# A written-out sequence in place of a priority planner: attention and linear attention, one core

## The chip, the cores and the metric

One core of one Trainium2 chip runs the whole kernel. The time is device microseconds of one execution, from its first instruction to its last; the median of several executions is given, with the lowest and the highest. A separate execution is taken by the hardware profiler, and all durations of single instructions come from that one. The engines are PE (TensorE, matmuls, with its weight loads shown as PEld), ACT (ScalarE), DVE (VectorE), POOL (GpSimd) and SP (SyncE, here only an issuer of DMA transfers).

## The reference

Two independent blocks, A and B, each take x (2048 rows, 640 columns, bf16) and weights wqkv (640 x 1920) and wo (640 x 640); their outputs are put side by side.

```python
# A: causal attention in a window of 256, 32 heads of 20
q, k, v = split(x @ wqkv)
scores = einsum("bhqd,bhkd->bhqk", q, k) * 20 ** -0.5
scores = where((i - j >= 0) & (i - j < 256), scores, -1e9)
a = (softmax(scores) @ v) @ wo
# B: linear attention, 32 heads of 20
phi = lambda t: where(t > 0, t + 1, exp(t)) + 1e-6
kv = einsum("bhsd,bhse->bhde", phi(k), v);  z = phi(k).sum(s)
b = (phi(q) @ kv / (phi(q) @ z + 1e-6)) @ wo
out = concatenate([a, b], axis=-1)
```

## The kernel before

The rows are cut into four tiles t of 512. For A and each t, the program makes q, k and v: `q{t}.{i}` and `k{t}.{i}` are groups of five matmuls of 512 columns (i from 0 to 4), `v{t}.{b}.{i}` are groups of five matmuls of 320 columns for each block b of 128 rows and each half i. The five matmuls of a group run over five pieces of 128 of the inner dimension, in order, and add up in one PSUM buffer F; there are four such buffers. An evacuation, named `.ev`, copies the finished buffer to SBUF, on ACT or on DVE.

The first tile of A is special. Its x is loaded row by row in four blocks, `x0n0` to `x0n3`, and PE transposes them (`x0t0` to `x0t3`, five matmuls each); v of block b needs only x0t{b}. Its weights come in pieces of 128 rows: `ld.wv0` to `ld.wv4` go straight to where they are used; `ld.wq0..4` and `ld.wk0..4` land in wqn and wkn and are rearranged by copies `cq0..5` and `ck0..5`. So matmul number c of a v group of this tile waits for wv{c}, and that of a q or k group for cq{c} or ck{c}. Before the data come, PE runs warm-up matmuls (`warm`, one piece of five with 512 columns and eight of two with 256). All later x tiles come by a transposing DMA (`ldxA1`, `ldxB0` and so on).

Attention of A goes by units `S{t}.{g}.{u}`: scores of eight heads go into the only score buffer S (four banks), ACT turns them into p by one exp `E{t}.{g}.{u}` (128 x 2048, in four cases 128 x 1536), DVE multiplies the edges by a mask (`M`), and after the units of a g, one `PV{t}.{g}` forms p times v in two F buffers. There are 76 units. The result goes to DRAM (`ow`), comes back turned (`oc`, and the sums `osum`), is normalised (`ln`, `rec`, `nrm`) and multiplied by wo (`oa{t}.{b}.{half}`), and stored. q and k also need copies of their heads in other partitions, which POOL's queue makes (`rl1`, `rl2`); v needs swapped halves (`sw`), by SP's queue.

B's work fills PE between the units: keys `kB{t}.{b}.{half}`, the sums `G` (16 matmuls each), `z`, `kv`, `kvwo`, and then queries `qB{t}.{c}`, denominators `den{t}` and outputs `ob{t}.{b}.{half}`. A last `flag` matmul counts bad sums; the engines read the flag at the very end and branch.

What sets the order. The function `build` only declares operations (some 2,080), each with the engines that could run it, a duration, its dependencies, a priority and, for some, an earliest time. The class `Planner` then plays this program through at build time: its `run` takes, again and again, the engine that is free first, and on it the ready operation of lowest rank; the operation is emitted there. PE's, ACT's, DVE's, POOL's and SP's streams and the one named ACTQ, transfers issued by ACT, are planned as six separate queues, although ACT and ACTQ are one stream of instructions on the chip. The priorities and the earliest times come from a table `TUNE` of numbers, the settings from `PRM`. Which of ACT and DVE does an evacuation also falls out of this play. On the chip, every engine then works its stream in order and waits on semaphores.

In order of issue the queues begin so, before:

- SP: wk2, wk1, x0n3, wq3, x0n2, wq1, x0n0, wv1, wq0, wq4, wq2, wv3, x0n1, xtok0, woA, wk0, wk4, wk3, ldxA1
- ACT: wv0, wv2, wv4 (loads), then the copies ck2, ck1, cq3, cq1, cq0, cq4, cq2
- PE: nine pieces of warm-up, x0t3, v0.3.1 (first matmul), v0.3.0, x0t2, v0.2.1, x0t0, and so on; all 40 v matmuls, 25 of q and 14 of k stand ahead of the first scores

Of the kernel before, what the change touches and what calls it, by code (L numbers as in the profile page):

```python
# [11 lines left out]
F32 = mybir.dt.float32  # L12
I32 = mybir.dt.int32
INF = 1 << 40
PRM = {"rq": "POOL", "pvw": 2854, "look": 13955, "slack": 991, "xm": 5, "sq": "SP"}
TUNE = {
# [49 lines left out]
}  # L66


def KEY(name, value):
# [25 lines left out]
ENGS = ["PE", "ACT", "DVE", "POOL", "SP", "ACTQ"]  # L95
# [5 lines left out]
class Planner:  # L101
# [54 lines left out]
                o.left += 1  # L156
            o.ready = {e: o.earliest for e in o.engs}

    def run(self, dry=False):
        self.prepare()  # L160
        avail = {e: [] for e in ENGS}
        for o in self.ops:
            if o.left == 0:
# [2 lines left out]
        free = self.free  # L166
        while True:
# [12 lines left out]
            t, e = best  # L180
# [6 lines left out]
            o = pick[1]  # L187
# [26 lines left out]
            done = t + dur  # L214
# [1149 lines left out]
```

## Time and profile before

| what | us |
|---|---|
| median of three runs | 260.22 |
| lowest, highest | 259.57, 260.45 |
| the profiled execution | 261.95 |
| its span, first to last instruction | 260.4 |
| PE busy | 245.7 |
| ACT busy | 198.6 |
| DVE busy | 181.5 |
| mean granted PE clock | 0.99 |

A row of the timeline has the start and the length in us, the engine, the line, the operation with what it writes and reads, the number of instructions merged into it, and in brackets the idle time before it and what ended that. SPq and ACTq are the issuing of transfers by SP and ACT. A row of the windows has the stretch, then for each engine its busy time and count, the granted PE clock (1.00 is full), the busy share of the DMA engines and GB/s. A group's row has its busy time, the mean length of one, the idle time before and what ended most of it. Line numbers of the program after the change are 70 higher in most of the file: line 416 becomes 486, 472 becomes 542, 568 becomes 638.

### The profile page before, as it was taken

The page shows a single profiled execution, that of the slowest core. Times are in us where ns is not written, and L with a number is a line of the kernel's source. Part 1 is how long each engine was busy: PE and PEld are TensorE (multiplying, and loading weights), DVE is VectorE, ACT ScalarE, POOL GpSimd, SP SyncE. Part 2 cuts the span into 40 slices and gives each one's busy share as a digit, 9 for nine tenths or more (in the row PEclk, how much of TensorE's full clock was granted, in tenths as well). Part 3 has the DMA queues.
Part 4 walks back from the last instruction along what each step waited for, and adds up shares of the span by engine and source line. Part 5 has one row for each costly group of instructions (what it writes and reads, how often), then busy time and mean ns, then how long its engine had stood idle before and what let it go on. Part 6 is the DMA issues. An engine that isn't in the chain of part 4 may idle for free.

```text
span 260.4 us, 9473 instructions
## 1 busy us (share of the span) xinstructions
PE 245.7 (94%) x4094; PEld 145.5 (56%) x4126; DVE 181.5 (70%) x458; ACT 198.6 (76%) x205; POOL 40.5 (16%) x93
## 2 busy tenths in 40 slices
PE   7699999999999999899999999999899999999993
PEld 4353455545555666545556666665545565556572
DVE  0456768978879987777778353459978777867831
ACT  4412789979789989977897778879979899756831
POOL 8000560009306300116041000000000000000000
PEclk9999999999999999999999999999979999999998
DMA  6769962786297816652457060662859223125133
GB/s 205 227 208 197 255 86 64 201 187 193 64 142 178 192 54 196 144 144 58 127 158 144 15 183 13 160 206 54 241 150 216 103 86 111 34 82 176 52 120 116
DMA packets 51828, 36.07 MB, mean 139 GB/s; under 512 B 31862, under 2 KB 50374, under 8 KB 51782
## 3 DMA queue, kind: packets, MB, share of 16 engines
q1 hardware_dynamic: 49302, 32.31, 47.0%
q0 software_dynamic: 2048, 2.63, 5.5%
q8 instruction: 33, 0.54, 0.9%
q10 hardware_dynamic: 432, 0.49, 0.7%
q14 instruction: 13, 0.11, 0.1%
HBM read 13.90 MB, written 10.26 MB: 93 GB/s over the span
## 4 chain that ended last, share of the span: by engine, by line
PE 79%; DMA 6%; ACT 5%; issue 3%; DVE 3%; SPq 2%; DVEq 0%
PE F L726 17%; PE F L507 14%; PE S L638 10%; PE F L864 9%; PE F L839 8%; PE F L1021 7%; PE F L568 7%; PE F L692 7%; ACT p L654 3%; DMA wkn<-in_A_wqkv_dram 2%; DMA wqn<-in_A_wqkv_dram 2%; PE F L1033 1%; DMA wv<-in_A_wqkv_dram 1%; ACT e L800 1%; SPq L1164 1%
## 5 line engine op out<-in xcount | busy, mean ns | idle before, releaser
L654 ACT ACTIVATE p<-S 128x2048 bf16<-128x2048 f32 x76 | 141.1, 1856 | 25.3 <-PE S L638 23.2
L666 DVE TENSOR_TENSOR p<-p,strip 128x256 bf16<-128x256 bf16 (+2 forms) x140 | 49.2, 379 | 9.5 <-ACT p L654 9.2
L800 ACT ACTIVATE e<-F 128x320 bf16<-128x320 f32 (+1 forms) x52 | 25.3, 500 | 5.8 <-PE F L1021 5.1
L416 DVE CAST even<-F 128x512 bf16<-128x512 f32 x30 | 20.7, 689 | 12.9 <-PE F L507 10.0
L839 PE MATMUL F<-wkB,xT 128*128 128x320 bf16 x160 | 27.9, 300 | 0.3 <-issue 0.2
L568 PE MATMUL F<-wv,xT 128*128 128x320 bf16 x160 | 26.3, 300 | 1.7 <-DVE xT L416 1.2
L538 POOL DMA_DIRECT2D odd<-even x32 | 17.0, 538 | 68.6 <-DVE even L416 30.1
L726 PE MATMUL F<-woA,oc 128*128 128x320 bf16 x160 | 26.5, 302 | 0.0
L1021 PE MATMUL F<-xT,wqB 128*128 128x512 bf16 x91 | 25.1, 394 | 1.1 <-issue 0.5
L507 PE MATMUL F<-xT,wk 128*128 128x512 bf16 x89 | 23.9, 380 | 1.4 <-issue 0.8
L416 DVE CAST osb<-F 128x320 bf16<-128x320 f32 x38 | 18.1, 486 | 10.2 <-PE F L726 9.8
L726 PE MATMUL F<-kvwo,pq 128*128 128x320 bf16 x160 | 24.9, 299 | 0.2 <-DVE p L666 0.2
L507 PE MATMUL F<-xT,wq 128*128 128x512 bf16 x92 | 24.0, 379 | 0.5 <-issue 0.3
L864 PE MATMUL F<-pk,xtok 128*128 128x320 bf16 x160 | 24.3, 300 | 0.0
L541 POOL DMA_DIRECT2D odd<-st x32 | 17.8, 562 | 27.3 <-DVE st L416 12.0
L692 PE MATMUL F<-p,sw 64*32 64x320 bf16 (+3 forms) x720 | 21.1, 254 | 0.0
L692 PE MATMUL F<-p,vt 64*32 64x320 bf16 (+3 forms) x720 | 21.0, 254 | 0.0
L416 DVE CAST ost<-F 128x512 bf16<-128x512 f32 x22 | 14.6, 687 | 8.8 <-PE F L692 8.7
L568 PEld LDWEIGHTS <-xT 128*128 128x128 bf16 x160 | 14.8, 98 | 9.6 <-DVE xT L416 1.8
L839 PEld LDWEIGHTS <-xT 128*128 128x128 bf16 x160 | 14.7, 98 | 9.0 <-issue 1.0
L726 PEld LDWEIGHTS <-oc 128*128 128x128 bf16 x160 | 15.1, 99 | 8.2 <-issue 1.3
L726 PEld LDWEIGHTS <-pq 128*128 128x128 bf16 x160 | 15.3, 98 | 7.8 <-issue 0.6
(87 smaller groups left out, 300.0 us busy)
## 6 DMA issues: line engine op xcount, KB each, us to landing
out_dram<-osb SPq DMA_DIRECT2D x32, 160.0 KB, 2.0
OD<-ost SPq DMA_DIRECT2D x32, 128.0 KB, 2.1
xtok<-in_B_x_dram SPq DMA_DIRECT2D x4, 640.0 KB, 5.3
oc<-OD SPq DMA_DIRECT2D x4, 640.0 KB, 4.3
odd<-even POOLq DMA_DIRECT2D x32, 48.0 KB, 3.8
sw<-vt SPq DMA_DIRECT2D x16, 87.0 KB, 2.7
odd<-st POOLq DMA_DIRECT2D x32, 32.0 KB, 2.9
wkn<-in_A_wqkv_dram SPq DMA_DIRECT2D x5, 160.0 KB, 5.8
```

The source lines that it names most:

```text
L416: nc.vector.tensor_copy(out=dst, in_=src)
L507: nc.tensor.matmul(ps[:, a:b], lhsT=w[:, kt, i, :], rhs=xb["t"][:, kt, a:b], start=(kt == 0), stop=(kt == KT - 1))
L568: return lambda ps: nc.tensor.matmul(ps[:], lhsT=xb["t"][:, kt, bb * P : bb * P + P], rhs=rhs_(), start=(kt == 0), stop=(kt == KT - 1))
L638: nc.tensor.matmul(st["s"][64 * i : 64 * i + 64, o0 : o0 + b - a], lhsT=kb["t"][32 * j : 32 * j + Dh, sl, ko : ko + 64], rhs=qb["t"][32 * ...
L654: nc.scalar.activation(out=o_, in_=i_, func=ACT.Exp, scale=scale)
L666: nc.vector.tensor_tensor(out=x, in0=x, in1=mkv[:, None, :].to_broadcast([P, 4, 64 * w]), op=ALU.mult)
L692: nc.tensor.matmul(O[i][32 * j : 32 * j + 32, a:b], lhsT=lhsT, rhs=pb["t"][64 * i : 64 * i + 64, o0 : o0 + b - a], start=(cnt == 0), stop= ...
L726: return lambda ps: nc.tensor.matmul(ps[:], lhsT=lhs(c), rhs=rhs(c, hf), start=(c == 0), stop=(c == KT - 1))
L800: nc.scalar.activation(out=eb["t"][:, 0:n], in_=ps[:], func=ACT.Exp)
L839: return lambda ps: nc.tensor.matmul(ps[:], lhsT=xb["t"][:, kt, b * P : (b + 1) * P], rhs=R["wkB"][:, kt, hf * HALF : (hf + 1) * HALF], st ...
L864: return lambda ps: nc.tensor.matmul(ps[:], lhsT=R["xt", tb // 4][:, tb % 4, c * P : (c + 1) * P], rhs=R["pk", tb // 4][:, tb % 4, hf * HA ...
L1021: return lambda ps: nc.tensor.matmul(ps[:], lhsT=R["wqB"][:, kt, :].rearrange("p (f c) -> p c f", c=KT)[:, c, :], rhs=xb["t"][:, kt, :], s ...
```

## The change

`PRM` and `TUNE` lose their contents (the settings fall back to defaults that are the same where they matter for what is built), and a list `SEQ` of 2,084 numbers comes in. Each number is an operation and its engine: `word // 8` is the operation's place in the order of declaration, `word % 8` the queue. A new method `follow` walks the list and emits each operation there; `run` calls it instead of the play. Which of the buffers F, O or L an operation gets now goes by who gave one back first in the list.

```diff
-PRM = {"rq": "POOL", "pvw": 2854, "look": 13955, "slack": 991, "xm": 5, "sq": "SP"}
-TUNE = {
-    "x0n0": -496785, "@x0n0": 5831, "x0n1": -176047, "@x0n1": 11250, "x0n2": -3061, "@x0n2": 4097, "x0n3": 93019, "@x0n3": 43, "ld.wv0": 41152,
...
-}
+PRM = {"sq": "SP"}
+TUNE = {}
+SEQ = [
+    100, 109, 32, 0, 368, 378, 141, 16, 40, 56, 24, 84, 76, 64, 336, 116, 132, 1344, 8, 188, 92, 212, 346, 196, 220, 320, 156, 330, 48, 281, 1136,
...
+]
...
+    def follow(self, dry):
+        done = set()
+        free = {}
+        for k in self.slots:
+            free.setdefault(k[0], []).append(k)
+        for word in SEQ:
+            o, e = self.ops[word // 8], ENGS[word % 8]
+            assert o.left == 0 and e in o.engs and o.idx not in done, o.name
+            done.add(o.idx)
+            if o.acq:
+                g, (n, kind) = o.acq
+                assert len(free[kind]) >= n, o.name
+                g["slot"] = [free[kind].pop(0) for _ in range(n)]
+            o.eng = e
+            if not dry:
+                o.emit(e)
+            self.log.append(o)
+            for g, i in o.rel:
+                free[g["slot"][i][0]].append(g["slot"][i])
+            for s in o.succ + o.osucc:
+                s.left -= 1
+        assert len(done) == len(self.ops)
+
     def run(self, dry=False):
         self.prepare()
+        if SEQ:
+            return self.follow(dry)
```

The operations are the same ones. What the list says, engine by engine:

- SP begins with x0n3, x0n1, x0n0, wv1, wv3, wk0, x0n2, wk3, wk1, wk4, wq1, wk2, wq0, wq3, wq4, wq2, ldxA1, sw0.0 (two), sw0.1, ldxB0, wkB; xtok0 and woA come later.
- ACT begins with the loads wv0 and wv4, the copy ck1, the load wv2, and then ck4 and evacuations; the other copies of wq and wk but cq4 are now DVE's.
- PE begins with a short piece of warm-up, the five long matmuls, x0t3, five short pieces, x0t1, v0.3.1 (first matmul), one piece, x0t0, one piece, v0.1.1, v0.3.1, v0.1.1, v0.0.0 (two), and then the third matmul of v0.3.1. Groups are mixed more finely: neighbours on PE belong to different groups 668 times, before 401 times. Ahead of the first scores stand 35 v matmuls and 35 of q and k.
- ACT has 214 operations and DVE 429, before 203 and 440: 80 evacuations and small operations stood on ACT between the exps, now 99.
- The flag matmul stands last on PE; before, 67 matmuls stood behind it.

140 rows, old and new, of tables (SEQ, TUNE) are left out of this document.

## The prediction

> **What bounds the kernel now.** I read the page's parts 1 and 5 first, then five-microsecond windows, then the timelines of the first 14 us and of the exps, and last the end of the chain.
>
> ```profile
> PE 245.7 (94%) x4094; PEld 145.5 (56%) x4126; DVE 181.5 (70%) x458; ACT 198.6 (76%) x205; POOL 40.5 (16%) x93
> ...
> L654 ACT ACTIVATE p<-S 128x2048 bf16<-128x2048 f32 x76 | 141.1, 1856 | 25.3 <-PE S L638 23.2
> ```
>
> ```profile
> 0.00:5.00 5.00, 3.51 (x12) 1.76 (x13) 0.28 (x2) 2.27 (x4) 3.86 (x24) 1.00 0.55 159
> 5.00:10.00 5.00, 2.99 (x26) 1.96 (x25) 0.98 (x2) 1.68 (x3) 1.84 (x5) 1.00 0.77 256
> 10.00:15.00 5.00, 4.23 (x36) 2.72 (x35) 2.78 (x8) 2.77 (x6) 0.00 (x0) 1.00 0.83 245
> ...
> 145.00:150.00 5.00, 5.00 (x149) 3.34 (x150) 1.99 (x6) 4.15 (x3) 0.00 (x0) 1.00 0.02 3
> ```
>
> PE is busy for 94% of the span. Of its 14.7 us idle, 4.3 lie in the first 15 us, and 4.1 behind its last matmul. In the middle two things run at the same pace: PE, and the ring scores, exp, next scores, since there is one score buffer. Its timeline:
>
> ```profile
> 26.21 1.88 ACT L654 ACTIVATE p<-S 128x2048 bf16<-128x2048 f32 x1 [0.67 <-PE S L638]
> 28.88 1.88 ACT L654 ACTIVATE p<-S 128x2048 bf16<-128x2048 f32 x1 [0.79 <-PE S L638]
> 31.45 1.88 ACT L654 ACTIVATE p<-S 128x2048 bf16<-128x2048 f32 x1 [0.70 <-PE S L638]
> ```
>
> An exp of 1.88 us and a gap of about 0.74, so 2.62 us per unit of scores. The gap takes one or two evacuations on ACT for nothing; a third costs time. The head:
>
> ```profile
> 1.38 0.06 DVE L437 MEMSET tiny<- 128x1 f32 x1
> ...
> 1.50 0.87 ACTq L472 DMA_DIRECT2D wv<-in_A_wqkv_dram  x2
> ...
> 2.40 0.45 ACTq L472 DMA_DIRECT2D wv<-in_A_wqkv_dram  x1
> ...
> 3.35 0.62 ACT L414 COPY wk<-wkn 128x512 bf16<-128x512 bf16 x1 [0.81 <-DMA wkn<-in_A_wqkv_dram]
> 4.83 0.33 SPq L1093 DMA_DIRECT2D x0n<-in_A_x_dram  x1
> 4.83 0.62 ACT L414 COPY wk<-wkn 128x512 bf16<-128x512 bf16 x1 [0.87 <-DMA wkn<-in_A_wqkv_dram]
> ...
> 7.38 0.33 SPq L472 DMA_DIRECT2D wv<-in_A_wqkv_dram  x1
> 7.41 0.45 PE L1126 MATMUL F<-ident,x0n 128*128 128x128 bf16 x5 [0.84 <-DMA x0n<-in_A_x_dram]
> ```
>
> and, from the chain that ended last, one load from its issue to its landing:
>
> ```profile
> 9.18 2.95 DMA wv<-in_A_wqkv_dram
> ```
>
> Three things are to be seen. First, loads are issued in order and held: the third x load went out when wk1 landed (SP and ACT both at 4.83), the next wv load when the first x load landed (7.38 and 7.41); the eight transfers in flight are reused in turn. Second, ACT's loads stand in ACT's own stream: they left at 1.50, when tiny was written (1.38 + 0.06), while SP issued from 1.04. Third, the first transfer issued landed at 3.35, the second at 4.75, the third of SP's queue at 7.4.
>
> **The change, part by part.** The page's execution took 261.95 us (span 260.4, 1.55 around it), 1.7 above the median of 260.22. I sum against the span and put the difference on the median.
>
> *Head.* x0n3, x0n1, x0n0 go first on SP, then wv1, wv3, wk0, x0n2, wk3, wk1. ACT issues wv0 and wv4 at once. But on ACT the copy ck1 of wk1 now stands ahead of the load of wv2, and every group of v needs wv2 as the third of its five weight pieces. PE takes its queue in order: three transposed blocks and six v matmuls, then v0.3.1's third, which waits for wv2. So:
> - x0n0, third on SP, lands at 6.7 to 7.4 (the row of 7.41, with one transfer less on ACT's queue).
> - wk1 reuses the place of x0n0, so it goes out then. A load issued at 7.75 landed by 10.21 (ACT's copy of wq0), the one at 9.18 in 2.95 us. wk1 lands at 9.7.
> - wv2 is issued at 9.75 and lands 2.95 us later: 12.7. Bounds: 11.9 with a landing of 2.3 us (the first load's, alone) and wk1 at 9.6; 14.2 with 4.4 (x0n1's under load).
> - From there to the first scores PE has 5 transposes, 29 v matmuls and 35 of q and k: 5 x 0.06 + 29 x 0.136 + 35 x 0.216 = 11.8 us (spacings from the runs of 11 at 12.17 and of 20 at 17.75), plus 0.3 of waits, as before's same stretch had (11.04 of work in 11.34).
> - Clock. PE stands still from about 9.5 to 12.7. The nearest row is the one place where PE was underused later:
>
> ```profile
> 189.00:190.00 1.00, 0.61 (x10) 0.25 (x17) 1.00 (x4) 1.00 (x3) 0.00 (x0) 1.00 0.39 133
> 190.00:191.00 1.00, 1.00 (x26) 0.54 (x23) 1.00 (x5) 1.00 (x3) 0.00 (x0) 0.54 0.00 0
> 191.00:192.00 1.00, 1.00 (x3) 0.29 (x2) 1.00 (x3) 1.00 (x1) 0.00 (x0) 0.50 0.58 137
> ```
>
> After 3.4 us with PE at 0.59 to 0.85 the granted clock was half for 3.4 us, which costs 1.7. The other bound is 0: from 7 to 10, at 0.41 to 0.56 busy, no drop shows. A PE that does nothing is nearer to the first, less what passes before wv2 lands: 1.6. First scores at 12.7 + 11.8 + 0.3 + 1.6 = 26.4, against 25.7: **+0.7**.
> The Trainium skill's page TensorE: Matmul & The Clock Gate (What's actually happening) says that the clock halves after at least one idle window of about 3.4 us, on a free-running grid. The row above dropped without an idle window. By the page a stop of 3.2 us need hold no whole window, and the head would be -0.9 instead of +0.7; that is rival 2.
>
> The other loads moved: xtok0 and woA leave the head (they put wk's last pieces at 16.00, which cost PE only a wait of 0.36). The first transposing load, whose issue holds SP for 5.55 us, now follows wq2 at about 11, and sw0.0, ldxB0 and wkB queue behind it. wkB then lands near 28; its first matmul stands four units, 10 us, behind the first scores. Nothing on the path; bounds 0 and the 0.36. POOL's relays keep their number and go by the evacuations; DVE's ck5 and cq5 (1.2 each) are done 8.7 us behind wv2, and q0.4 asks for them at 11.6: hidden, 0.
>
> *Middle.* From first to last scores there are 75 units. For each I take the larger of the PE work standing between its scores and the next, and 1.88 (1.45 for the four short exps) plus the larger of 0.74 and ACT's other work between the two exps, at the rows' durations less 0.05 each for overlap. Before this sums to 200.5 where the trace has 224.2 - 25.7 = 198.5, so it is fair to 1% and the bias is common. After, it sums to 203.2: **+2.7**. The terms: PE work 190.3 to 193.2, as five v matmuls and some of k0 move behind the first scores and work comes forward from the end; ACT's work between exps 40.3 to 48.8, as 19 more evacuations of 0.43 to 0.58 move there. DVE loses 7 us there, but at 70% it bounds nothing. Bounds for what such a sum can't see (a buffer freed late, a mask behind a waiting evacuation): -2 (nearly half of the 5.8 us of PE idle in before's middle gone) and +3 (each t losing as much as S3.1 did over its sum, 0.6, and one dip of the clock more). I take 0, as before's sixteen groups of units each came out within 0.6 of the sum.
>
> *End.* PE work from the last scores on falls from 31.6 to 30.2: **-1.4**. The flag matmul moves from 246.9 to PE's very end: 0.17 of PE, 0.15 and 0.14 of DVE, and SP's read of 0.54. The last evacuation (0.43) and store issue (0.4) take as long, and SP reads the flag behind them anyway: 0, at most 0.3.
>
> Sum: 0.7 + 2.7 - 1.4 = **+2.0 us**, or 262.2 on the median. The break-even is first scores at 24.4.
>
> **The rivals.**
> 1. *wv2 does not wait.* If a load on ACT leaves without waiting for ck1, or ck1 is early, wv2 goes out at 2.40 as the third load of before did and lands by 8.0 (5.6, the longest landing of a wv load there). PE reaches that point at about 9.4 (strip is ready at 3.1, then five warm-up matmuls of 0.43, ten of 0.1 to 0.2, three blocks), first scores at 9.4 + 12.1 = 21.5: -4.2 + 2.7 - 1.4 = -2.9, 257.3. For: x and wv do lead the queues. Against: the 1.50 row. It decides once wv2 lands before 10.7 at half clock or 12.3 at full clock. Then the change would have done what its words say; by my reading four of five pieces of wv lead, and the fifth does not.
> 2. *The clock stays up*, as it did from 7 to 10 with PE at 0.41 to 0.56. Against: here PE does not run at all, and 190 shows that less was enough. Head -0.9, sum +0.4, 260.6: within 0.3% (0.8 us, about what a measurement of this kernel can tell from no change).
> 3. *The middle suffers more.* ACT's added evacuations hold the ring and buffers beyond the sum, +2 to +3: about 264.5. For: two gaps with three evacuations, where before has none. Against: PE's queue is spaced to 2.6 us there.
> 4. *The middle gains* the -2 above, with PE's stall at 186 to 190 and its clock dip gone: 260.2, or faster with an early wv2.
>
> **Chances.** Forecast 0.46; rival 1 0.20; rival 2 0.13; rival 3 0.12; rival 4 0.09, shared between same and faster. Rival 2 also spills over to faster with wv2 at 11.9. Hence faster 0.28, same 0.14, slower 0.58. The range for 8 in 10 is 257.2 to 264.4, from rival 1 to rival 3; the forecast's own is 261.0 to 263.6.
>
> **What would show it.** On ACT the load of wv2 starts at 9.5 or later, right when wk1 lands; PE idle 2.5 us or more ahead of a v matmul (F<-wv,xT) that waits for DMA wv; a granted clock of half in the slices behind it; first scores at 25 to 27.5, last scores near 228; ACT's idle ahead of the exps down from 25 by about 6; and PE's last matmul 32 us behind the last scores. An ACT load of wv2 issued before 3 us, or first scores before 23, would make me wrong in the head; 75 units taking under 199 or over 204 us, in the middle.

## The result and the profile after

| | before | after |
|---|---|---|
| median, us | 259.89 (258.89 to 260.45, four executions) | 272.32 (271.54 to 273.88, four executions) |
| the profiled execution, its span | 261.95, 260.4 | 271.54, 270.0 |

The changed kernel takes 1.049 times as long (95% interval 1.043 to 1.056): slower, by 12.4 us where the prediction had 2.0 and a range that ended at 264.4. The page's part 1 and its group of the exps, after:

```profile
PE 246.4 (91%) x4097; PEld 146.3 (54%) x4126; DVE 176.6 (65%) x447; ACT 200.8 (74%) x216; POOL 40.9 (15%) x93
...
L724 ACT ACTIVATE p<-S 128x2048 bf16<-128x2048 f32 x76 | 141.2, 1858 | 21.9 <-PE S L708 19.0
```

The engines have little more work: PE went from 245.7 to 246.4 us, ACT from 198.6 to 200.8. Of the 9.7 us of span, 9.0 are idle time of PE (14.7 before, 23.6 after). ACT's idle time ahead of the exps (the number behind the second bar) fell from 25.3 to 21.9 all the same. I cut both spans at three marks (first exp, last exp, end of PE's last matmul):

| stage, us | before | after | difference |
|---|---|---|---|
| start to first exp | 26.21 | 26.46 | +0.25 |
| first to last exp (75 units) | 198.55 | 203.26 | +4.7 |
| last exp to PE's end | 31.5 | 30.6 | -1.0 |
| PE's end to the span's end | 4.1 | 9.8 | +5.7 |

The spans differ by 9.7 us, the medians by 12.4. The execution profiled before was 2.1 us longer than the median of its kernel. It holds the stretch at half clock at 190 that the prediction shows; two other executions of this order or nearly this order, without such a stretch, took 197.0 and 196.8 us from first to last exp (the order before written out, and the flag late, in the table below). Against those the middle lost 6.3 us, not 4.7. The execution profiled after was the shortest of its four, 0.8 below their median; where the others lost more was not profiled.

**Head.** From the timeline after (start, length, engine, line, operation, count, idle time before it and what ended it):

```profile
6.15 2.34 PE L1139 MATMUL F<-strip,ident 128*128 128x256 bf16 x10
9.12 0.62 ACT L484 COPY wk<-wkn 128x512 bf16<-128x512 bf16 x1 [6.59 <-DMA wkn<-in_A_wqkv_dram]
9.13 0.35 ACTq L542 DMA_DIRECT2D wv<-in_A_wqkv_dram  x1
9.63 4.85 SPq L553 DMA_TRANSPOSE xT<-in_A_x_dram  x1
14.10 1.66 PE L638 MATMUL F<-wv,xT 128*128 128x320 bf16 x11 [3.45 <-DMA wv<-in_A_wqkv_dram]
26.46 1.88 ACT L724 ACTIVATE p<-S 128x2048 bf16<-128x2048 f32 x1 [1.31 <-PE S L708]
```

The wait is where the prediction put it: the load of wv2 leaves with the copy that waits for wk1, and PE stands 3.45 us for it. Eleven matmuls in 1.66 us, 0.136 apart, are full speed: the clock did not fall here. The +0.25 at the first exp is less than this mark varies by: in three other executions with the same head (flag early, the two swap runs) it came at 25.8, 25.2 and 27.7. Part of that is PE's warm-up. The ten small matmuls at 6.15 took 2.34 us here, 0.21 apart, and 1.34 us, 0.11 apart, in others, while the windows show a granted clock of 1.00 for both.

**Middle.** Nearly all of the +4.7 lies in one place. The timeline of 99 to 112:

```profile
99.43 1.88 ACT L724 ACTIVATE p<-S 128x2048 bf16<-128x2048 f32 x1
99.66 0.44 SPq L927 DMA_DIRECT2D xtok<-in_B_x_dram  x1
100.60 0.65 SPq L653 DMA_DIRECT2D sw<-vt  x1
101.97 1.88 ACT L724 ACTIVATE p<-S 128x2048 bf16<-128x2048 f32 x1
103.03 2.86 SPq L553 DMA_TRANSPOSE xT<-in_A_x_dram  x1
105.85 0.49 DVE L486 CAST vt<-F 128x320 bf16<-128x320 f32 x1 [3.88 <-DMA sw<-vt]
106.40 0.43 PE L909 MATMUL F<-wkB,xT 128*128 128x320 bf16 x2 [2.72 <-DVE vt L486]
107.26 1.88 ACT L724 ACTIVATE p<-S 128x2048 bf16<-128x2048 f32 x1 [3.08 <-PE S L708]
111.85 1.88 ACT L724 ACTIVATE p<-S 128x2048 bf16<-128x2048 f32 x1 [0.67 <-PE S L708]
```

The exps are 2.54 apart until 101.97, and then 5.29 and 4.59. DVE's cast at 105.85 is the evacuation of the v group v2.1.0. It waits 3.88 us for a transfer that reads the tile it writes, the second half of the swap `sw2.0`, issued at 100.60; PE waits behind the cast, and the scores behind PE. The chain that ended last gives the transfer's time, and that of the late load in the head:

```profile
9.13 4.92 DMA wv<-in_A_wqkv_dram
...
100.60 5.16 DMA sw<-vt
```

In the kernel before, the evacuation of v2.1.0 was planned ahead of both halves of that swap; in the written list the second half stands ahead of it. By the code the two do not even touch the same columns (the swap's half reads columns 336 to 683 of both blocks, the evacuation writes into columns 0 to 335 of the second), but the program makes the later one in the list wait. The second long gap, 4.59, is mostly the clock (in the run with the flag early, where the wait was shorter and the clock stayed up, it was 3.37). Windows of 1 us (stretch, busy time and count of PE, PEld, DVE, ACT and POOL, granted clock, share of the DMA engines, GB/s):

```profile
107.00:108.00 1.00, 0.90 (x20) 0.44 (x5) 1.00 (x4) 0.74 (x1) 0.00 (x0) 0.90 1.17 355
108.00:109.00 1.00, 0.58 (x3) 0.20 (x2) 0.96 (x3) 1.00 (x1) 0.82 (x2) 0.50 0.12 42
109.00:110.00 1.00, 1.00 (x6) 0.52 (x5) 0.52 (x2) 0.20 (x2) 1.00 (x3) 0.50 0.36 57
110.00:111.00 1.00, 1.00 (x5) 0.56 (x4) 0.55 (x2) 0.64 (x2) 1.00 (x3) 0.50 0.66 90
```

**The span's end.** PE's last matmul, the flag's, is issued at 260.12. What reads its result, by the views of the flag's tile and of the lines that use it (lengths in ns, least, median and most, then the starts of first and last), after:

```profile
L1276 DVE CAST fint<-fsum x1: 141/141/141, 260.5 to 260.5; 1x1 int32<-1x1 f32 x1
L1288 POOLq TENSOR_LOAD <-fint x1: 770/770/770, 260.7 to 260.7; - x1
L1289 POOLq INC_SWDGE_SEM  x1: 1471/1471/1471, 262.4 to 262.4; - x1
L1429 POOLq DRAIN  x3: 34/107/5288, 263.9 to 269.8; - x3
```

and the same before:

```profile
L1206 DVE CAST fint<-fsum x1: 141/141/141, 247.8 to 247.8; 1x1 int32<-1x1 f32 x1
L1218 POOLq TENSOR_LOAD <-fint x1: 491/491/491, 248.0 to 248.0; - x1
L1219 POOLq INC_SWDGE_SEM  x1: 1471/1471/1471, 249.5 to 249.5; - x1
L1359 POOLq DRAIN  x3: 34/107/5288, 251.0 to 260.1; - x3
```

POOL reads the flag, branches, spends 1.47 us on one instruction and 5.29 us in a DRAIN. Before, it began this at 248.0 and its long DRAIN was over at 256.3, with PE's last matmul. After, it begins at 260.7 and nothing covers it.

### The profile page after: what moved, and what is told of

Its sections match the earlier page's. It is cut to its first block, busy times and chain, and to the rows that moved or that the text cites. A ratio compares the mean times of both kernels' runs of the same rounds, so it can differ in the third digit from the quotient of the medians.

```text
span 270.0 us, 9475 instructions
## 1 busy us (share of the span) xinstructions
PE 246.4 (91%) x4097; PEld 146.3 (54%) x4126; DVE 176.6 (65%) x447; ACT 200.8 (74%) x216; POOL 40.9 (15%) x93
## 4 chain that ended last, share of the span: by engine, by line
PE 76%; DMA 8%; ACT 5%; DVE 4%; issue 2%; SPq 1%; DVEq 0%; ACTq 0%
PE F L796 16%; PE F L577 15%; PE S L708 9%; PE F L638 8%; PE F L909 7%; PE F L1091 7%; PE F L934 5%; PE F L762 5%; DMA sw<-vt 3%; ACT p L724 3%; DMA wv<-in_A_wqkv_dram 2%; PE F L1103 2%; DMA x0n<-in_A_x_dram 1%; DMA wkn<-in_A_wqkv_dram 1%; DVE p L736 1%
## 5 line engine op out<-in xcount | busy, mean ns | idle before, releaser
L724 ACT ACTIVATE p<-S 128x2048 bf16<-128x2048 f32 x76 | 141.2, 1858 | 21.9 <-PE S L708 19.0
L736 DVE TENSOR_TENSOR p<-p,strip 128x512 bf16<-128x512 bf16 (+2 forms) x140 | 49.7, 382 | 18.7 <-ACT p L724 18.3
L909 PE MATMUL F<-wkB,xT 128*128 128x320 bf16 x160 | 32.8, 308 | 3.3 <-DVE vt L486 2.7
L638 PE MATMUL F<-wv,xT 128*128 128x320 bf16 x160 | 31.1, 300 | 3.6 <-DMA wv<-in_A_wqkv_dram 3.5
L796 PE MATMUL F<-woA,oc 128*128 128x320 bf16 x160 | 30.6, 303 | 0.6 <-ACT osb L484 0.5
L577 PE MATMUL F<-xT,wk 128*128 128x512 bf16 x91 | 26.7, 380 | 0.7 <-issue 0.5
L796 PE MATMUL F<-kvwo,pq 128*128 128x320 bf16 x160 | 27.3, 299 | 0.1
L577 PE MATMUL F<-xT,wq 128*128 128x512 bf16 x92 | 26.8, 380 | 0.3
L608 POOL DMA_DIRECT2D odd<-even x32 | 17.1, 541 | 58.3 <-ACT even L484 39.4
L486 DVE CAST ost<-F 128x512 bf16<-128x512 f32 x28 | 18.5, 685 | 9.2 <-PE F L762 9.0
L638 PEld LDWEIGHTS <-xT 128*128 128x128 bf16 x160 | 14.7, 98 | 12.3 <-issue 4.7
L874 DVE TENSOR_SCALAR e<-e 128x320 bf16<-128x320 bf16 (+1 forms) x52 | 13.5, 259 | 10.8 <-ACT e L870 9.9
L486 DVE CAST even<-F 128x512 bf16<-128x512 f32 x21 | 14.5, 688 | 8.7 <-PE F L577 8.0
```

What stands on the lines that cost most here:

```text
L486: nc.vector.tensor_copy(out=dst, in_=src)
L577: nc.tensor.matmul(ps[:, a:b], lhsT=w[:, kt, i, :], rhs=xb["t"][:, kt, a:b], start=(kt == 0), stop=(kt == KT - 1))
L638: return lambda ps: nc.tensor.matmul(ps[:], lhsT=xb["t"][:, kt, bb * P : bb * P + P], rhs=rhs_(), start=(kt == 0), stop=(kt == KT - 1))
L724: nc.scalar.activation(out=o_, in_=i_, func=ACT.Exp, scale=scale)
L736: nc.vector.tensor_tensor(out=x, in0=x, in1=mkv[:, None, :].to_broadcast([P, 4, 64 * w]), op=ALU.mult)
L796: return lambda ps: nc.tensor.matmul(ps[:], lhsT=lhs(c), rhs=rhs(c, hf), start=(c == 0), stop=(c == KT - 1))
```

## The experiments

The runs are told by the cost they test. An entry of the list is moved by a helper at the end of the changed kernel, so that all line numbers stay:

```diff
+def move(word, before):
+    SEQ.remove(word)
+    SEQ.insert(SEQ.index(before), word)
```

The stages of every profiled execution, for reference below (us; the last four rows are told last):

| kernel | first exp | first to last exp | last exp to PE's end | to the span's end | span |
|---|---|---|---|---|---|
| before | 26.2 | 198.6 | 31.5 | 4.1 | 260.4 |
| after | 26.5 | 203.3 | 30.6 | 9.8 | 270.0 |
| flag early | 25.8 | 200.9 | 30.0 | 5.1 | 261.8 |
| swap behind the evacuation | 25.2 | 198.4 | 30.2 | 9.8 | 263.5 |
| xtok1 behind the swap | 27.7 | 198.8 | 30.4 | 9.7 | 266.6 |
| wv2 early | 21.6 | 204.4 | 30.3 | 9.8 | 266.0 |
| wv2 later still | 30.4 | 202.1 | 30.4 | 9.8 | 272.6 |
| all three moves | 21.6 | 198.5 | 30.3 | 5.1 | 255.5 |
| all three moves, last stores spread | 22.9 | 198.4 | 30.0 | 5.2 | 256.5 |
| before, flag late | 25.4 | 196.8 | 31.8 | 9.5 | 263.5 |
| the order before, written out | 25.3 | 197.0 | 31.8 | 4.3 | 258.3 |
| head alone | 24.2 | 204.3 | 31.8 | 4.1 | 264.3 |
| head alone, mended | 22.0 | 200.8 | 31.8 | 4.4 | 258.9 |
| the rest alone | 26.5 | 198.6 | 30.3 | 4.5 | 260.0 |

### The flag early

The first two entries are the counts, the other three the flag's steps on DVE, PE and DVE.

```diff
+move(12858, 15418)
+move(12866, 16130)
+move(16650, 16130)
+move(16656, 13104)
+move(16666, 12986)
```

> The changed kernel with the two counts of zero weights (L846) and the flag's three steps moved forward in its order: the counts ahead of and behind the last B query evacuations, the flag's matmul ahead of the last A output groups. Theory A (a fixed chain of POOL's behind the flag's branch): the span ends 4 us behind PE's last matmul, as it did before, in place of 9.7: about -5.6 us against the changed kernel, some 266.7 us, 1.027 times the kernel before; POOL's 5.29 us DRAIN starts near 252 in place of 263.9. Theory B (the prediction's: the stores end the program whatever the flag does): PE's end moves by 0.2 us at most and the span's end with it, 271.9 to 272.5 us. What would spoil A in part: 1.6 us of DVE work ahead of the last normalizations, which could cost up to 0.7 us at PE's end.

Measured: 265.07 us (263.32 to 267.63), 1.023 times (1.016 to 1.029).

```profile
251.49 5.19 PE L796 MATMUL F<-kvwo,pq 128*128 128x320 bf16 x37
...
L1429 POOLq DRAIN  x3: 34/107/5288, 249.5 to 261.6; - x3
```

POOL's DRAIN now starts at 249.5 beside PE's last matmuls, and the span ends 5.1 us behind PE in place of 9.8. That is 4.6 of the 5.7; the other 1.1 stays, and what causes it was not found. The median fell by 7.2, more than the stage explains: here the same cast waited 2.73 us for the swap, not 3.88, and the clock stayed up. Theory B, which was the prediction's own, is out.

### The flag late in the kernel before

The same cost from the other side, one edit to the kernel before. With it the planner also moves seven other matmuls near the end and gives four evacuations to the other engine of ACT and DVE:

```diff
-    f2 = pl.op({"PE": 60}, flag_mm, -250000, [f1], slots=(1, "F"), g=fg, name="flag2")
+    f2 = pl.op({"PE": 60}, flag_mm, -250000, [f1], slots=(1, "F"), g=fg, name="flag2", earliest=400000)
```

> The kernel before with one thing changed: the flag's matmul may only come as the last on PE, as the change puts it, while the two counts and the flag's first step on DVE stay where they were; everything else stays with the priorities (a dozen matmuls near the end change places). Theory A (POOL's fixed chain): POOL reads the flag at about 256.6 in place of 248.0 and needs 1.5 us for one step and 5.29 for its DRAIN behind it, so that the span ends some 9.5 us behind PE's end in place of 4.1: about +5.4 us, 265.6 us, 1.021 times. Theory B (the prediction's 0, at most 0.3): 260.2 to 260.5 us.

Measured: 265.41 us (264.63 to 267.51), 1.025 times (1.020 to 1.030): +5.6 us.

```profile
253.83 0.17 PE L1197 MATMUL F<-bad,ones 128*1 128x8 bf16 x1
...
L1218 POOLq TENSOR_LOAD <-fint x1: 482/482/482, 254.4 to 254.4; - x1
L1359 POOLq DRAIN  x3: 34/107/5288, 257.4 to 263.2; - x3
```

From PE's end to the span's end it is 9.5 us, as after the change (9.8). PE's work behind the last exp takes 31.8 us against 31.5, so the reordered matmuls are not what costs the time. One instruction of 0.17 us, moved to the end of PE's stream, costs 2% of this kernel. This is shown from both sides.

### The swap behind the evacuation

```diff
+move(4308, 3912)
```

> The changed kernel with one entry moved: the second half of the swap sw2.0 stands behind the evacuation of v2.1.0 in the order, not ahead of it. SP's own order stays the same, only who waits for whom turns round. Theory A (the evacuation waits for a transfer that reads its tile): the wait of 3.88 us ahead of the cast at 105.85 goes, the exps stay 2.6 us apart between 102 and 112 (they were 5.3 and 4.6), PE's clock does not fall to 0.50 at 108 to 110, and the last exp comes 4 to 4.7 us sooner: some 267.9 us, 1.031 times the kernel before. Theory B (what is short at 100 to 106 is the transfer itself, behind 640 KB of xtok1): the swap now starts later, lands at 106 to 108, and the PV matmuls that read it wait in the evacuation's place: 0 to -2 us. Theory C (the wait goes but the half clock has another cause): -2.7 us.

Measured: 266.93 us (265.02 to 267.99), 1.028 times (1.023 to 1.033).

```profile
100.70 1.88 ACT L724 ACTIVATE p<-S 128x2048 bf16<-128x2048 f32 x1
100.90 0.49 DVE L486 CAST vt<-F 128x320 bf16<-128x320 f32 x1 [0.20 <-PE F L638]
101.88 0.65 SPq L653 DMA_DIRECT2D sw<-vt  x1
103.11 1.88 ACT L724 ACTIVATE p<-S 128x2048 bf16<-128x2048 f32 x1 [0.21 <-PE S L708]
```

The cast waits for PE's matmuls only, the swap leaves behind it, the exps stay 2.4 to 2.6 apart, and 75 units take 198.4 us: 4.9 less. No instruction changed its place on any engine or queue. Only who waits for whom was turned round. Theory A; B and C are out.

### xtok1 behind the swap

```diff
+move(5580, 3912)
```

> The changed kernel with the load of xtok1 (640 KB) moved behind the second half of the swap sw2.0 on SP; the swap itself stays ahead of v2.1.0's evacuation in the order, so that the evacuation still has to wait for it. Theory A (both together make the stall: the order makes the wait, the 640 KB ahead of the swap its length): the swap leaves at 99.7 and lands after 2.3 to 3 us (its other three took about 2.3) at 102 to 102.7, the cast waits 0.3 to 0.9 us in place of 3.88, the exps at 102 to 112 come 2.6 to 3.4 apart, no half clock: -3.5 to -4.5 us, some 268.3 us (1.032). Theory B (the transposing load at 103 is what slows the swap): the swap lands within 0.5 us of where it did and the stall stays: 0 to -1 us. Loading xtok1 3 us later should cost nothing: its readers come 10 us later at the least, by the trace of the changed kernel.

Measured: 267.56 us (265.61 to 268.08), 1.029 times (1.024 to 1.033).

```profile
101.24 0.64 SPq L653 DMA_DIRECT2D sw<-vt  x1
102.33 0.39 SPq L927 DMA_DIRECT2D xtok<-in_B_x_dram  x1
103.78 0.49 DVE L486 CAST vt<-F 128x320 bf16<-128x320 f32 x1 [0.62 <-DMA sw<-vt]
...
13.62 2.70 PE L638 MATMUL F<-wv,xT 128*128 128x320 bf16 x11 [3.74 <-DMA wv<-in_A_wqkv_dram]
```

The dependence is still there, but without 640 KB ahead of it the swap lands 2.5 us after its issue, and the cast waits 0.62 us. 75 units take 198.8. So the stall had two causes, and taking away either is enough: the order made the wait, the load ahead of the swap its length.

The last line is the head of the same order as after, and it went otherwise: eleven matmuls took 2.70 us, not 1.66, and windows of 0.2 us show the clock at 0.50 from 14.1 to 17.5. First exp at 27.65. So the half clock that the prediction charged to the head does occur there, in some executions.

### wv2 early

```diff
+move(125, 281)
```

> The changed kernel with the load of the third block of wv ahead of the first wk copy on ACT, so that it leaves when ACT's other loads leave and not at 9.13. Theory A (the prediction's step on the head): the 3.45 us in which PE waits for wv at 10.65 to 14.10 go, first exp at 22.9 to 23.5 in place of 26.46, about -3 us in all: 269.2 us, 1.036 times the kernel before. Theory B (something else stands right behind: other loads are pushed back by 160 KB, near 0.5 us each, or wq and wk come too late for the projections): first exp at 24.5 to 26, -0.5 to -2 us. Theory C (the exps of the middle lose again what the head gained, since what paces them is PE's and the buffers' work): first exp sooner by 3 us, last exp by less than 1.

Measured: 267.07 us (265.99 to 267.58), 1.026 times (1.021 to 1.030).

```profile
2.39 0.45 ACTq L542 DMA_DIRECT2D wv<-in_A_wqkv_dram  x1
...
6.08 1.34 PE L1139 MATMUL F<-strip,ident 128*128 128x256 bf16 x10
...
21.57 1.88 ACT L724 ACTIVATE p<-S 128x2048 bf16<-128x2048 f32 x1 [1.31 <-PE S L708]
...
97.09 1.88 ACT L724 ACTIVATE p<-S 128x2048 bf16<-128x2048 f32 x1
103.33 1.88 ACT L724 ACTIVATE p<-S 128x2048 bf16<-128x2048 f32 x1 [4.04 <-PE S L708]
```

PE has no wait left from 10 us to the first scores, and the first exp comes 4.9 us sooner. Not all of that is the move's. The ten warm-up matmuls took 1.34 us in this execution and 2.34 in the one after the change, so PE's first v matmul began at 7.54 and not at 8.81. From that matmul to the first scores it is 13.5 us in place of 17.2: the move is worth 3.6 us, the wait of 3.45 and little else. The last run with all moves, whose warm-up took 2.34 us again, has its first exp at 22.9, also 3.6 ahead of after. The stall in the middle is untouched and a little longer (6.24 and 4.43 between exps). Theory A, with about the gain that it gave.

### wv2 later still

The wait made longer, by a second wk copy and a wq copy ahead of the load on ACT:

```diff
+move(148, 125)
+move(172, 125)
+move(180, 125)
+move(305, 125)
+move(257, 125)
```

> The changed kernel with the wait in the head made longer: on ACT, the load of wv's third block stands behind one more wk copy and a wq copy, so that it leaves when wq's block has landed, near 12.3, and not at 9.1. PE idles some 6 to 6.8 us in place of 3.45. Theory A (as in the stalls at 106 and 102 of the runs before, where 2.7 us without work was followed by 3.4 us at half clock and 3.2 us by 6.5: a longer idle time brings the clock down in the head too): +3.2 us for the wait and +1.7 to 3.3 for the clock: 277 to 279 us, 1.066 to 1.073. Theory B (the clock does not fall in the head): +2.7 to 3.3 us and PEclk at 1.00 through 10 to 26: 275 to 275.6 us, 1.058. Theory C (the head's wait is partly covered: the middle gives some back): less than +2.5.

Measured: 273.86 us (273.45 to 276.51), 1.055 times (1.048 to 1.062); by its time alone not told apart from the changed kernel.

```profile
12.21 0.33 ACTq L542 DMA_DIRECT2D wv<-in_A_wqkv_dram  x1
...
16.58 3.08 PE L638 MATMUL F<-wv,xT 128*128 128x320 bf16 x11 [7.27 <-DMA wv<-in_A_wqkv_dram]
...
14.00:16.00 2.00, 0.00 (x0) 0.00 (x0) 0.00 (x0) 0.00 (x0) 0.00 (x0) 0.50 1.17 284
```

PE stood still from 9.31, the clock was at half from 12.7 to 19.5, and the first exp came at 30.37, 3.9 later than after. From the first v matmul to the first scores it is 5.2 us longer than after: 3.8 more of wait, and about 1.4 for the half clock once PE worked again. So the mechanism of A is there. The sum is not: the median rose by 1.5, which is in theory C's range. In the profiled execution the warm-up was 1.0 shorter than in the one after the change, and 75 units took 1.1 less, as the swap's wait happened to be 2.62 us. This run says what the head costs the head, and not what it costs the whole.

### All three moves

> All three moves together. If the three costs are separate (theory A of each): -5.6 - 4.4 - 3 = -13 against the changed kernel, 259.3 us, level with the kernel before (0.99 to 1.003). If they overlap, or if the middle takes back what the head gives, 261 to 264 us. If the order written out has a further cost that these three hide, above 264.

Measured: 257.52 us (256.97 to 259.19), 0.992 times (0.989 to 0.995), so faster than the changed kernel, and 0.8% faster than the one before. By the medians the three single runs sum to -17.8 (7.2, 5.4, 5.2) and this is -14.8; by the stages that each move acts on it is 4.6 + 4.9 + 4.9 = 14.4 against 14.6 in the spans. The stages add up; the 1.3 us of the head that came from the short warm-up are on both sides. The medians do not, probably because the swap's wait varied between executions (2.62 to 4.34 us in the four profiles that have it) and went along with the others; only one execution of each run was profiled, so this is not shown. The three costs are separate and, together, are more than the whole loss.

One more move, to spread the last stores:

```diff
+move(16616, 16202)
+move(16624, 16202)
+move(16633, 16202)
+move(16644, 16202)
```

> The run with all three moves, and one more: the last two matmuls of B's output group ob3.3.1, its evacuation and its store stand right behind the group's first three matmuls, not among the last groups, so that only two stores and not three leave in the last 3 us (the last store took 1.34 us to issue there, 0.33 us in the kernel before). Theory A (the last store queues behind the two ahead of it): PE's end to the span's end 4.1 to 4.4 us in place of 5.1, 256.6 to 257.2 us, 0.988 to 0.991 times the kernel before. Theory B (the last store's own landing sets the end): no difference, 257.5 us, 0.992.

Measured: 257.58 us (257.03 to 260.95), 0.990 times (0.987 to 0.992). The last store still took 0.93 us to issue, and PE's end to the span's end 5.2 us: no difference that can be measured from the run without it.

### Where the gain over the kernel before comes from

First the form alone, the kernel before with its own order written out:

> The kernel before with its own order written out entry by entry and followed, nothing moved: only PSUM slots are handed out in the order they come free. Theory A (writing it out costs nothing; all that the change moves in time is where the entries stand): 260 us, 0.997 to 1.003. Theory B (slots handed out in another way, or the missing clock of the planner, cost something): above 1.005.

Measured: 260.85 us, 1.002 times (0.9995 to 1.005). Writing the order out costs nothing that can be told apart; what moves the time is the order. Then each half of the order with all three moves, with the order before for the rest. The run's list is written out; it is the one that these lines give, with the changed list, wv2 early, as `SEQ` and the order before as `BEFORE`:

```diff
+head = SEQ[:134]
+SEQ = head + [w for w in BEFORE if w // 8 not in {x // 8 for x in head}]
```

> The head of the changed kernel alone, with wv's third block sent early (the run before), on the rest of the order of the kernel before: the first 134 entries, up to the last evacuation ahead of the first score, are the changed order's; all that follows stands as the priorities of the kernel before put it. Theory A (the head's gain is a shift): first exp at 21.6 in place of 26.2, first to last exp still 198.5, the end as before: -4.6 us, 255.6 us, 0.982 times the kernel before. Theory B (the kernel before did more of its projections ahead of the first exp, and what is left has to be done under the exps): first to last exp longer by 1 to 3 us, 256.6 to 258.6 us. Theory C (it takes all back): 260.

Measured: 260.75 us, 1.006 times (1.003 to 1.010), as theory C had it. The profiled execution was the longest of nine, 265.84 us, and shows a seam:

```profile
24.00 7.33 SPq L553 DMA_TRANSPOSE xT<-in_B_x_dram  x1
...
39.18 1.51 PE L909 MATMUL F<-wkB,xT 128*128 128x320 bf16 x5 [5.09 <-DMA xT<-in_B_x_dram]
```

PE's stream was earlier (first exp at 24.2), SP's list of loads was not, and so PE waited 5.09 us for B's first strip. Whether the shorter executions had this wait too is not known. With it mended (the first score, its exp and that load in the head, wkB behind them):

> The head alone again, with the seam of the last attempt mended: there the transposing load of B's first strip left at 24.0, behind five other loads, and PE waited for it 5.1 us; and the first score stood behind more projections, as in the kernel before. Here the prefix runs through the first score and its exp, the transposing load is in it, and the load of wkB stands right behind. Theory A (a shift): first exp at 21.6, first to last exp 198.5 as in the kernel before: 255.6 us, 0.982. Theory B (PE work that the kernel before did ahead of the first exp is now done under the exps, at the place where PE is full): the first 15 exps take 39.0 us in place of 37.3, or more; 257 to 259 us, 0.988 to 0.996. Theory C (the rest of that order does not suit an earlier head: loads and swaps come late by its list): 260 or more.

Measured: 260.54 us, 1.002 times (1.000 to 1.004). First exp at 22.0, 3.3 sooner than with the order before written out, and 75 units in 200.8 us, 3.8 more. Of these, 2.1 lie in the first 15 units (39.4 against 37.3), nearly all of it between the first exp and the second, where PE has 0.46 us of idle time and does projections that stood ahead of the first exp; another 1.4 in the last 15 units, which hold a stretch at half clock at 188; the profiled execution of the kernel before has one at 190 too. By its median this is theory C, by the first 15 units the mechanism of B: a head that is 3.3 us shorter by moving work behind the mark is no gain.

> The other half: the kernel before up to its first exp (152 entries), then the changed order with the flag early and the swap behind the evacuation. If the parts add up as the run with all three moves shows them (first to last exp 198.46 against 198.55, last exp to PE's end 30.35 against 31.55, PE's end to the span's end 5.1 against 4.1): -0.3 us, 259.9 us, 0.999 times. If the refined order of the middle is worth something on its own that the earlier head hid: 256 to 258.5. If it only suits the head it was refined with: above 261.

Measured: 261.16 us, 1.004 times (1.000 to 1.008), just above the bound of the third forecast. Against the order before written out, PE's last stretch is shorter by 1.4 us, the middle longer by 1.6; the head, the same order, took 1.3 more in this execution. So neither half gains anything, and both together gain 0.8%. Against the order before written out, the run with all three moves has -3.7 in the head, +1.4 in the middle, -1.4 in the last stretch and +0.8 at the end. By these single executions the middle pays once for work from both sides, where each half alone paid in full (2.1 and 1.6). Why it would pay only once was not settled.

## Why the prediction was wrong, point by point

- **Direction and first step right.** "On ACT the copy ck1 of wk1 now stands ahead of the load of wv2": wk1's landing forecast at 9.7, was 9.1; wv2 issued at 9.75, was 9.13; first scores at 26.4, were at 25.96. That the sum came so close is luck: two of its terms were off, one each way. wv2 took 4.92 us to land and not 2.95 (the upper bound was 4.4), with the transposing load issued half a microsecond behind it, which the text placed at 11. And the clock term of 1.6 was not paid in the profiled execution, as rival 2 had it, but was in another of the same order of the head. Rival 1 fell with the row of 9.13. What it said of an early wv2 held: with wv2 issued at 2.39 and the other two faults mended, the kernel is faster than before.
- **Middle, the sum.** The sum of the larger of PE work and the ring gave +2.7. With the stall gone, 75 units take 198.4, against 197.0 in an execution of the order before without a clock dip and 198.6 in the one used for the forecast. So +1.4 or less, where the text had +2.7. The 203.3 that was measured lies inside the prediction's 199 to 204 by luck: the loss was not the added work of the sum but a single stall.
- **Middle, what the sum can't see.** The failed step is "The other loads moved ... Nothing on the path" together with the bound of +3 for "a buffer freed late, a mask behind a waiting evacuation". One wait of 3.88 us and a half clock behind it cost 4.9. It could have been read off the list: the second half of sw2.0 stands 35 entries ahead of an evacuation into its tile, and directly behind the load of xtok1. I looked through the transfers for late arrivals. I did not look for what has to wait until a transfer has finished reading.
- **End.** Last exp to PE's end: -1.4 forecast, -1.0 measured.
- **Flag.** "0, at most 0.3", because "SP reads the flag behind them anyway": the step that failed worst: the flag's early place is worth 4.6 us in the changed kernel and 5.4 in the one before (5.6 on its median). SP reads it late, and so do ACT and DVE. POOL is the one that read it early, at 248.0, and had 8.3 us of its own to do from there. I took the last reader for the only one that counts.
- **Rival 3** forecast the size of the middle's loss, but by another cause (more evacuations on ACT). Added ACT work was no part of it: the swap run leaves all of that in place. There, ACT's idle time ahead of the exps is 18.5, 6.8 below that of before (forecast: about 6), and costs nothing.

Of the 9.7 us of span, 5.7 lie behind PE's end (4.6 of them the flag, 1.1 of open cause), 4.7 in the middle and 0.25 in the head, less 1.0 between the last exp and PE's end. The flag's 4.6 and the stall's 4.9 together are 9.5; they carry the miss.

## What to carry to other kernels

In a written order, every pair of entries is a possible wait: for each transfer look not only at who needs what it brings, but at who may not write until it has read, and what stands ahead of it in its queue. An instruction that every engine reads at the end has as its cost the longest chain behind any of its readers, so list the readers engine by engine and see which had started early. And a time gained ahead of a mark is only worth what remains when the work pushed behind the mark has been paid.

## What was not expected of the hardware

- POOL needs a fixed time behind the final branch: 1.47 us and a DRAIN of 5.29 us, the same within 0.01 us in all the executions profiled here. With its read of the flag and its branch that is 8.3 us before (248.0 to 256.3) and 8.5 after (260.7 to 269.2). It is hidden only if the flag is known that long before the other engines end.
- PE's warm-up. In executions with the same order of PE's head the same ten matmuls of the warm-up took 2.34, 1.89, 1.79 or 1.34 us, and the first exp moves with them. The granted clock of the windows does not show it. What decides it was not found.
- The clock. Every stretch at half clock ahead of PE's last matmul lasted about 3.4 us (107.8 to 111.2 after, 190.1 to 193.5 before, 14.1 to 17.5 in the xtok1 run) or twice that (101.6 to 108.4 with wv2 early, 12.7 to 19.5 with wv2 later still). In the head, idle times of 2.78, 2.83 and 3.45 us brought no fall, 3.74 and 7.27 did; in the middle, 1.57 did not, and 1.46 (wv2 later still, where the clock fell at 111.6), 2.72 and 3.18 did. So the idle time's length does not decide by itself. The Trainium skill, TensorE: Matmul & The Clock Gate (What's actually happening), says that activity is judged in windows of 3.4 us that run free of the kernel: the lengths of the stretches agree, and so does the head. The falls after 1.46, 2.72 and 3.18 us do not fit its condition of an idle window, and neither does the one at 190 before, with PE busy for 0.59 to 0.85: some work in a window is evidently too little. How much was not measured.
- One load of 160 KB took 2.95 us to land in the kernel before and 4.92 with a transposing load issued 0.5 us behind it; a swap of 87 KB took 5.16 us right behind a load of 640 KB and at most 2.5 with that load moved behind it. That the transposing load slows the first was not tried by itself.
